# The first batch's keys and queries loaded as twelve rows a partition, in a block-sparse attention feeding a mixture of experts

## The chip, the cores and the metric

The kernel runs on one core of one Trainium2 chip. Its metric is the device time in microseconds of one execution, as the median of several runs. The core has five engines with a queue of instructions each: TensorE (PE in the profile, its weight loads PEld), VectorE (DVE), ScalarE (ACT), GpSimd (POOL), and SyncE (SP), which here issues most of the transfers. Transfers run on 16 DMA engines that all the queues share. A matmul writes to PSUM; ACT and DVE copy results from there to SBUF.

## What is computed

Attention over 4 batches of 8 heads, 768 positions of 64 elements, with a mask in blocks of 32 positions: a query block sees its neighbours, the first and last block, and three sampled blocks; the first and last query blocks see everything. The result, as 3,072 tokens of 512, goes to the best of 8 experts.

```python
scores = scale * np.matmul(q, k.transpose(0, 1, 3, 2))
mask = np.abs(blk_i - blk_j) <= window
mask = mask | (blk_i == 0) | (blk_j == 0) | (blk_i == n_blocks - 1) | (blk_j == n_blocks - 1)
for qb in range(n_blocks):
    for kb in sampled_blocks[qb]:
        mask[qb * block:(qb + 1) * block, kb * block:(kb + 1) * block] = True
attn = np.exp(np.where(mask, scores, -1e9) - max)   # and divided by its sum
x = np.matmul(attn, v)                              # to (tokens, 512)
expert = np.argmax(x @ w_gate, axis=1)
y = gate_weight * (np.maximum(x @ w1[expert], 0) @ w2[expert])
```

## The kernel before

The two halves follow one another: attention until about 280 us of the profiled execution, then the experts. In the attention each batch needs its keys and queries with the head's 64 elements on the partitions. They come from memory with positions on the partitions and are turned on TensorE. Two heads make a pair; a batch has four pairs (NPR), so 64 + 64 partitions hold the two heads of a pair.

`fill_stage` (L137) loads keys or queries of one pair into a staging buffer by two DMAs, one a head, each with position 128 c + p of chunk c on partition p; a partition gets six pieces of 64 fp32 elements (256 B each) a head. There are two staging slots for keys and two for queries, used by pairs in turn. `turn` (L150) makes twelve transposes of 64 positions by 128 columns (both heads at once) into a PSUM tile `tp` of two banks, and `turned` (L159, the copy at L161) copies 128x768 to the place where the pair's keys or queries lie, one instruction: on ACT for the first batch's keys, on DVE for its queries. The copy writes runs of 64 elements.

The first batch is brought in ahead of the regular steps. Its values come by `load_v` (L142, copies at L144): a DMA per head, also in pieces of 256 B. `keep_v` (L146, L148) writes them back to memory as whole rows of all heads (v_rows, 2,080 B a row), from which GpSimd gathers the sampled blocks' rows by indirect DMA (`fetch_values`, L488) and SP fetches the two end blocks (`fetch_ends`, L496). v_rows has to be complete before either reads it.

For the first and last query blocks, which see all keys, `scores(plan_all(0, pr))` multiplies (24 matmuls at L321), ACT takes the Exp (L331), and `attend_all` multiplies the result with the values (twelve second products a pair, L355) into an accumulator that the regular steps finish. `make_masks` (L243) makes the masks and the row numbers for the gathers (rows_of, L248; mask, L254) from four small matmuls. These PSUM tiles (tp, s, fl) share three buffers of two banks, in the order of allocation.

The order of all this is written out by hand: in this part of the program each engine executes in the order in which the code issues. Before, a loop over the pairs runs: turn keys, turn queries, load the pair two further on into the freed slot, (after the first pair) load the values' second half, (after the second pair) write v_rows and load the gate, scores and Exp of this pair, (after the second pair) masks, second products of the pair before. Twenty-two transposes of the identity (L240) at the very start keep TensorE busy until the first data are there.

The regular steps then take a query group and two pairs each; a step's scores need copies of the sampled keys (kr, L528) and end keys (xk, L512 and L513), and its second products need the gathered values (around). `not_before` (L500) paces the gathers.

Of the kernel before, what the change touches and what calls it, by code (L numbers as in the profile page):

```python
# [7 lines left out]
F32 = mybir.dt.float32  # L8
# [9 lines left out]
def kernel(  # L18
# [11 lines left out]
    nc = tc.nc  # L30
    P = 128
    B, H, S, D = q.shape
# [3 lines left out]
    NCH = S // P  # L36
    CW = NCH // 2 * P
    NPR = H // 2
# [32 lines left out]
    ident = const.tile([P, P], F32, name="ident")  # L71
# [14 lines left out]
    upper, lent = {}, ExitStack()  # L86
# [25 lines left out]
    def held(flat):  # L112
        a, c = NPR * S, 2 * NPR * S
        return (
            flat[:, :a].rearrange("p (r s) -> p r s", r=NPR), flat[:, a:c].rearrange("p (r s) -> p r s", r=NPR),
            flat[:, c : c + NCH * VR].rearrange("p (c w) -> p c w", c=NCH),
        )

    sets = [held(other[:]), held(room[:])]
    sets = [sets[(b + B - 1) % 2] for b in range(B)]  # L120
    at = 2 * NPR * S + NCH * VR
    stage = [[room[:, at + (2 * i + j) * S : at + (2 * i + j + 1) * S] for i in range(2)] for j in range(2)]
# [14 lines left out]
    def fill_stage(b, pr, which, slot=0):  # L137
        to = stage[which][slot].rearrange("p (c h d) -> p c h d", c=NCH, h=2)
        for hh in range(2):
            nc.sync.dma_start(to[:, :, hh, :], (k, q)[which][b, 2 * pr + hh].rearrange("(c p) d -> p c d", p=P))  # L140

    def load_v(b, hs=None):  # L142
        for h in range(H) if hs is None else hs:
            nc.sync.dma_start(sets[b][2][:, :, h * VW : h * VW + D], v[b, h].rearrange("(c p) d -> p c d", p=P))  # L144

    def keep_v(b, cs=None):  # L146
        for c in range(NCH) if cs is None else cs:
            nc.sync.dma_start(v_d[b][c * P : (c + 1) * P, :], sets[b][2][:, c, :])  # L148

    def turn(b, pr, which, on=None, slot=0):  # L150
        src = stage[which][slot].rearrange("p (c w) -> p c w", c=NCH)
        tp = upper["ps_s"].tile([P, 2, 512], F32, name="tp", tag="s")
        for c in range(NCH):
            for j in range(2):
                r = slice(j * D, (j + 1) * D)
                nc.tensor.transpose(tp[:, j, c * D : (c + 1) * D], src[r, c, :], ident[r, r])
        return lambda: turned(b, pr, which, on, tp)

    def turned(b, pr, which, on, tp):  # L159
        to = sets[b][which][:, pr, :].rearrange("p (c j t) -> p j c t", c=NCH, j=2)  # L160
        (on or nc.scalar.copy)(to, tp[:, :, : NCH * D].rearrange("p j (c t) -> p j c t", c=NCH))  # L161
# [81 lines left out]
    def make_masks(spread, whose, own, qb):  # L243
        fl = upper["ps_s"].tile([P, 2, 2, NTI], F32, name="fl", tag="s")
        for w in range(2):
            for ch in range(2):
                nc.tensor.matmul(fl[:, w, ch, :], lhsT=spread[:, w, ch, :], rhs=whose[:], start=True, stop=True)
        nc.vector.tensor_scalar(  # L248
            rows_of.rearrange("p (t c) -> p c t", c=2), fl[:, 0], scalar1=float(BLK), scalar2=qb[:, 2:3], op0=ALU.mult, op1=ALU.add,
        )  # L250
        for ch, p0 in ((0, D), (1, 0)):
            for ti in range(2):
                shape = [P - p0, NG - ti, 2, BLK]
                nc.vector.tensor_tensor(  # L254
                    mask[p0:, : NG - ti, 1 + ch, ti, :].rearrange("p t (a i) -> p t a i", a=2),
                    fl[p0:, 1, ch, ti::2].unsqueeze(2).unsqueeze(3).to_broadcast(shape),
                    own[p0:, ch, :].unsqueeze(1).unsqueeze(3).to_broadcast(shape), op=ALU.mult,
                )
# [6 lines left out]
        nc.gpsimd.memset(two.rearrange("p c (h w) -> p c h w", w=VW)[:, :, :, D], 1.0)  # L265
    for pr in range(2):
        for which in range(2):
            fill_stage(0, pr, which, pr)
    load_v(0, range(4))
    make_lists_pool = ExitStack()  # L270
    lists = make_lists(make_lists_pool.enter_context(tc.tile_pool(name="mk", bufs=1)))
    rt = {}
    xbs, xos, lgs, banks_of, es = {}, {}, {}, {}, {}
# [8 lines left out]
    def all_queries(b, pr):  # L282
        return lambda r: sets[b][1][:, pr, :].rearrange("p (n i) -> p n i", i=BLK)[r, :: NB - 1, :]

    def at_cols(tile_, a, n):
        return lambda r: tile_[r, a : a + n]
# [13 lines left out]
    def plan_all(b, pr):  # L300
        kT = sets[b][0][:, pr, :]
        return [(j, at_cols(kT, c * P + j * D, D), all_queries(b, pr), c * D, D) for c in range(NCH) for j in range(2)], []
# [11 lines left out]
    def scores(*plans):  # L314

        ss = [upper["ps_s"].tile([P, 2, 512], F32, name="s") for _ in plans]
        for s, (few, _) in zip(ss, plans):
            for j, keys, queries, a, n in few:
                for hh in range(2):
                    r = slice(hh * D, (hh + 1) * D)  # L320
                    nc.tensor.matmul(s[j * D : (j + 1) * D, hh, a : a + n], lhsT=keys(r), rhs=queries(r), start=True, stop=True)  # L321
        for s, (_, many) in zip(ss, plans):
            for keys, queries, a, n in many:
                for hh in range(2):
                    r = slice(hh * D, (hh + 1) * D)
                    nc.tensor.matmul(s[:, hh, a : a + n], lhsT=keys(r), rhs=queries(r), start=True, stop=True)  # L326
        found = []
        for s in ss:
            e = ea[:, units[0] % NE, :].rearrange("p (h w) -> p h w", h=2)
            units[0] += 1  # L330
            nc.scalar.activation(e, s[:, :, : 6 * D], AF.Exp, scale=scale)  # L331
            found.append(e)
        return found
# [18 lines left out]
    def product(b, g, pr, ti, hh, e, values, last):  # L352
        bank, begun = bank_of(b, g, pr)
        op = bank[:, : 4 * (D + 4)].rearrange("p (r h w) -> p r h w", r=2, h=2)
        nc.tensor.matmul(  # L355
            op[ti * D : (ti + 1) * D, pr % 2, hh, : D + 1], lhsT=e, rhs=values[:, (2 * pr + hh) * VW : (2 * pr + hh + 1) * VW],
            start=ti not in begun, stop=last, skip_group_check=True,
        )
        begun.add(ti)
# [12 lines left out]
    def attend_all(b, pr, e, chunks):  # L372
        for c in chunks:
            for hh in range(2):
                product(b, GL, pr, 1, hh, e[:, hh, c * D : (c + 1) * D], sets[b][2][:, c, :], c == NCH - 1)
# [9 lines left out]
            attend_all(b, pr, e_all, range(3, NCH))  # L385


    for pr in range(NPR):
        turn(0, pr, 0, None, pr % 2)()
        turn(0, pr, 1, nc.vector.tensor_copy, pr % 2)()  # L390
        if pr + 2 < NPR:
            fill_stage(0, pr + 2, 0, pr)
            fill_stage(0, pr + 2, 1, pr)
        if pr == 0:
            load_v(0, range(4, H))
        if pr == 1:
            keep_v(0)
            nc.sync.dma_start(wg[:], moe_w_gate.rearrange("(c p) e -> p c e", p=P))
        (es[("all", pr)],) = scores(plan_all(0, pr))
        if pr == 1:  # L400
            make_masks(*lists)
            make_lists_pool.close()
        if pr > 0:
            attend_all(0, pr - 1, es[("all", pr - 1)], range(NCH))
    attend_all(0, NPR - 1, es[("all", NPR - 1)], range(NCH))
    wp = ctx.enter_context(tc.tile_pool(name="wp", bufs=1))
    sm = ctx.enter_context(tc.tile_pool(name="sm", bufs=1))
    work = ctx.enter_context(tc.tile_pool(name="work", bufs=2))
# [194 lines left out]
    def attention_again():  # L603
        oh, pen = dense_tables(small)
        for b in range(B):
            for two in (sets[b][2],):
                nc.gpsimd.memset(two.rearrange("p c (h w) -> p c h w", w=VW)[:, :, :, D], 1.0)
            load_v(b)
            for pr in range(NPR):
                for which in range(2):  # L610
                    fill_stage(b, pr, which)
                    turn(b, pr, which)()
            for g in range(NG):
                for pr in range(NPR):
                    shifted(b, g, pr, oh, pen)
                    if pr % 2:
                        divide(b, g, pr // 2)
                turn_out(b, g)
                logits(b, g)
            gate(b)  # L620
            gate_weights()
# [913 lines left out]
```

## Time and profile before

| | us |
|---|---|
| median of three runs | 679.02 (676.74 to 680.68) |
| the profiled execution | 650.76 |
| its span, first to last instruction | 649.0 |
| TensorE busy, matmuls | 611.7 (94% of the span) |
| VectorE busy | 300.9 (46%) |
| ScalarE busy | 218.1 (34%) |
| TensorE busy in the first 35 us | 27.0 |
| DMA share and rate in the first 35 us | 0.94, 199 GB/s |

Durations below come from the profiled execution. A row of the timeline gives the start, the time that the merged instructions took, the engine and line, the tiles written and read, the count, and in brackets how long the engine had been idle and what ended it. Queues carry a q (SPq); a transfer's row there is its issue, not its data. A fp32 matmul shows as two instructions. The row of a stage gives its busy time per engine, the clock that TensorE was granted as a share of full speed, the mean busy share of the 16 DMA engines, and the rate.

### The profile page before, as it was taken

How to read it: one execution, taken by the hardware profiler on the slowest of the kernel's cores; microseconds unless marked ns; L12 is line 12 of the kernel's file. 1: busy time of each engine (PE TensorE's matmuls, PEld its weight loads, DVE VectorE, ACT ScalarE, POOL GpSimd, SP SyncE). 2: the span in 40 equal slices, each digit the busy share in tenths (PEclk: the TensorE clock that was granted, in tenths of full speed). 3: DMA queues.
4: the chain of work that ended last, by engine and by line, in shares of the span. 5: the costliest groups of instructions: out<-in, count | busy, mean ns of one | idle time of the engine just before them, and what ended most of it. 6: DMA issues, size and time to landing. Idle time of an engine off the chain costs nothing. (4 is left out here: it accounts for less than half of the span.)

```text
span 649.0 us, 21354 instructions
## 1 busy us (share of the span) xinstructions
PE 611.7 (94%) x8952; PEld 512.0 (79%) x8952; DVE 300.9 (46%) x966; ACT 218.1 (34%) x418; POOL 184.1 (28%) x289
## 2 busy tenths in 40 slices
PE   7789999998999997999999999999989999999994
PEld 6778888997999886987777777877869678867862
DVE  4247765765577488734920495202091024602200
ACT  2347755775677655431111011111111211111110
POOL 2047753552455344620111221011400212020210
PEclk9689999999999999699999999999999999999998
DMA  9889886987797338876888999869995799989950
GB/s 184 210 195 245 243 218 158 221 231 198 158 232 235 95 90 290 283 260 231 315 299 299 335 383 348 293 239 382 396 397 192 256 405 397 339 278 402 396 189 20
DMA packets 136249, 170.93 MB, mean 263 GB/s; under 512 B 83444, under 2 KB 83445, under 8 KB 136118
## 3 DMA queue, kind: packets, MB, share of 16 engines
q1 hardware_dynamic: 126080, 137.61, 65.4%
q0 software_dynamic: 10000, 31.59, 15.2%
q8 instruction: 80, 1.31, 0.9%
q14 instruction: 51, 0.42, 0.2%
q10 hardware_dynamic: 38, 0.00, 0.0%
HBM read 150.11 MB, written 19.33 MB: 261 GB/s over the span
## 5 line engine op out<-in xcount | busy, mean ns | idle before, releaser
L1094 PEld LDWEIGHTS hp<-around,room 128*128 128x128 f32 x1216 | 138.3, 192 | 7.3 <-issue 5.1
L1094 PE MATMUL hp<-around,room 128*128 128x128 f32 x1216 | 140.8, 276 | 1.4 <-ACT kr L1101 1.4
L1075 DVE STREAM_TRANSPOSE around<-xg 32x128 f32<-32x128 f32 x208 | 63.0, 303 | 125.9 <-PE hp L1094 95.9
L1108 PE MATMUL zp<-room,kr 128*128 128x512 f32 x256 | 112.7, 594 | 0.0
L488 POOL DMA_INDIRECT around<-v_rows,rows_of x88 | 92.6, 1052 | 63.5 <-DVE xk L513 25.3
L331 ACT ACTIVATE ea<-s 128x768 f32<-128x768 f32 x104 | 79.7, 809 | 91.1 <-PE s L326 70.7
L355 PE MATMUL op<-around,ea 128*64 128x65 f32 x2112 | 87.6, 228 | 5.2 <-DMA around<-v_rows,rows_of 3.9
L1108 PEld LDWEIGHTS zp<-room,kr 128*128 128x128 f32 x256 | 47.6, 191 | 54.6 <-issue 54.6
L355 PEld LDWEIGHTS op<-around,ea 128*64 128x64 f32 x2112 | 76.3, 140 | 13.3 <-DMA around<-v_rows,rows_of 4.5
L337 DVE TENSOR_TENSOR ea<-ea,mask 128x768 f32<-128x768 f32 x80 | 73.2, 954 | 14.8 <-ACT ea L331 14.8
L1101 ACT ACTIVATE kr<-hp 128x512 f32<-128x512 f32 x36 | 21.5, 597 | 117.4 <-PE hp L1094 109.9
L1123 POOL DMA_INDIRECT out_dram<-kr,sB x14 | 14.1, 1005 | 164.7 <-ACT kr L1113 106.1
L1113 ACT ACTIVATE kr<-zp,xg 128x512 f32<-128x512 f32 x16 | 11.0, 687 | 101.2 <-PE zp L1108 101.2
L1201 DVE STREAM_TRANSPOSE ea<-ea 32x128 f32<-32x128 f32 x84 | 21.7, 285 | 32.7 <-DMA ea<-x_rows,gB 32.0
L321 PE MATMUL s<-room 64*64 64x64 f32 x736 | 24.4, 237 | 5.3 <-DVE room L161 4.6
L1123 POOL DMA_INDIRECT out_dram<-kr,sA x5 | 5.1, 1020 | 79.6 <-ACT kr L1113 79.6
L326 PE MATMUL s<-other,kr 64*128 64x64 f32 x352 | 26.9, 266 | 0.7 <-issue 0.7
L321 PEld LDWEIGHTS s<-room 64*64 64x64 f32 x736 | 20.2, 147 | 7.3 <-issue 4.5
L326 PE MATMUL s<-room,kr 64*128 64x64 f32 x352 | 25.8, 261 | 0.0
L326 PEld LDWEIGHTS s<-other,kr 64*128 64x128 f32 x352 | 25.0, 195 | 0.8 <-issue 0.8
L326 PEld LDWEIGHTS s<-room,kr 64*128 64x128 f32 x352 | 23.9, 190 | 1.0 <-issue 1.0
L500 POOL COPY paced<-sums 1x1 f32<-1x1 f32 x42 | 7.5, 179 | 60.1 <-DVE sums L415 55.6
(338 smaller groups left out, 870.2 us busy)
## 6 DMA issues: line engine op xcount, KB each, us to landing
room<-in_moe_w_dram SPq DMA_DIRECT2D x46, 2048.0 KB
room<-in_moe_w_dram SPq DMA_DIRECT2D x16, 512.0 KB
room<-in_k_dram SPq DMA_DIRECT2D x32, 192.0 KB
room<-in_q_dram SPq DMA_DIRECT2D x32, 192.0 KB
x_rows<-xb SPq DMA_DIRECT2D x20, 256.0 KB
v_rows<-room SPq DMA_DIRECT2D x12, 260.0 KB
v_rows<-other SPq DMA_DIRECT2D x12, 260.0 KB
room<-in_v_dram SPq DMA_DIRECT2D x16, 192.0 KB
```

The costliest lines, as they stand in the source:

```text
L321: nc.tensor.matmul(s[j * D : (j + 1) * D, hh, a : a + n], lhsT=keys(r), rhs=queries(r), start=True, stop=True)
L326: nc.tensor.matmul(s[:, hh, a : a + n], lhsT=keys(r), rhs=queries(r), start=True, stop=True)
L331: nc.scalar.activation(e, s[:, :, : 6 * D], AF.Exp, scale=scale)
L337: nc.vector.tensor_tensor(e, e, m[:, None, :].to_broadcast([P, 2, 6 * D]), op=ALU.mult)
L355: nc.tensor.matmul(op[ti * D : (ti + 1) * D, pr % 2, hh, : D + 1], lhsT=e, rhs=values[:, (2 * pr + hh) * VW : (2 * pr + hh + 1) * VW], sta ...
L488: nc.gpsimd.indirect_dma_start(out=around[p0:, par, 1 + ti + 2 * ch, :], out_offset=None, in_=v_d[b][:, :], in_offset=bass.IndirectOffsetO ...
L1075: nc.vector.transpose(xT[d, :, t], xg[t, :DM].rearrange("p (c q) -> p c q", c=DB)[:, :, d])
L1094: nc.tensor.matmul(hp[:, m, :], lhsT=st[i]["w1"][:, c, fb * P : (fb + 1) * P], rhs=st[i]["xT"][:, c, :], start=(c == 0), stop=(c == DB - 1),)
L1101: nc.scalar.activation(hT[:, g * (FB // 2) : (g + 1) * (FB // 2), :], hp[:], AF.Relu)
L1108: nc.tensor.matmul(zp[:], lhsT=st[i]["hT"][:, fb, :], rhs=st[i]["w2"][:, fb, :], start=(fb == 0), stop=(fb == FB - 1),)
L1123: ins = nc.gpsimd.indirect_dma_start(out=to[:, :], out_offset=bass.IndirectOffsetOnAxis(ap=at, axis=0), in_=rows, in_offset=None, bounds_c ...
L1201: nc.vector.transpose(xT_u[d, :, j * P + tq * 32 : j * P + (tq + 1) * 32], xg_u[t, j, :DM].rearrange("p (c q) -> p c q", c=DB)[:, :, d],)
```

## The change

The first batch's keys and queries are loaded otherwise, turned otherwise, and the order of the opening is another. Later batches keep `fill_stage` and `turn`.

A pair's two heads lie in memory one after the other, so the whole pair is one contiguous block. `fill_rows` loads it by one DMA: partition h * 64 + i takes positions 12 i to 12 i + 11 of head h, 768 elements or 3,072 B in one piece. `turn_rows` again makes twelve transposes of 64 by 128, now one for each head and each two neighbouring positions, so that a PSUM bank holds one head: the even position's elements on partitions 0 to 63, the odd one's on 64 to 127. Four copies of 64x384 put them in the order of positions: bank 0 (the first head) by ACT, bank 1 by DVE, even and odd each. A copy reads PSUM with a step of 64 elements (six of them, then the next) and writes to SBUF with a step of two elements.

```diff
+    KG = S // D
+
+    def fill_rows(b, pr, which, slot):
+
+        nc.sync.dma_start(stage[which][slot], (k, q)[which][b, 2 * pr : 2 * pr + 2].rearrange("h (i j) d -> (h i) (j d)", j=KG))
+
+    def turn_rows(b, pr, which, slot):
+        src = stage[which][slot]
+        tp = upper["ps_s"].tile([P, 2, 512], F32, name="tp", tag="s")
+        for hh in range(2):
+            r = slice(hh * D, (hh + 1) * D)
+            for j in range(KG // 2):
+                nc.tensor.transpose(tp[:, hh, j * D : (j + 1) * D], src[r, j * P : (j + 1) * P], ident[r, r])
+        for hh, copy in enumerate((nc.scalar.copy, nc.vector.tensor_copy)):
+            to = sets[b][which][hh * D : (hh + 1) * D, pr, :].rearrange("p (i j a) -> p a i j", j=KG // 2, a=2)
+            for a in range(2):
+                copy(to[:, a], tp[a * D : (a + 1) * D, hh, : KG // 2 * D].rearrange("p (j i) -> p i j", i=D))
...
-            fill_stage(0, pr, which, pr)
+            fill_rows(0, pr, which, pr)
...
-    for pr in range(NPR):
-        turn(0, pr, 0, None, pr % 2)()
-        turn(0, pr, 1, nc.vector.tensor_copy, pr % 2)()
+    def turn_first(pr):
+
+        for which in range(2):
+            turn_rows(0, pr, which, pr % 2)
         if pr + 2 < NPR:
-            fill_stage(0, pr + 2, 0, pr)
-            fill_stage(0, pr + 2, 1, pr)
-        if pr == 0:
+            for which in range(2):
+                fill_rows(0, pr + 2, which, pr)
+        if pr == 1:
             load_v(0, range(4, H))
-        if pr == 1:
             keep_v(0)
             nc.sync.dma_start(wg[:], moe_w_gate.rearrange("(c p) e -> p c e", p=P))
+
+    def scores_first(pr):
         (es[("all", pr)],) = scores(plan_all(0, pr))
-        if pr == 1:
-            make_masks(*lists)
-            make_lists_pool.close()
-        if pr > 0:
-            attend_all(0, pr - 1, es[("all", pr - 1)], range(NCH))
-    attend_all(0, NPR - 1, es[("all", NPR - 1)], range(NCH))
+
+    turn_first(0)
+    turn_first(1)
+    scores_first(0)
+    turn_first(2)
+    scores_first(1)
+    turn_first(3)
+    make_masks(*lists)
+    make_lists_pool.close()
+    scores_first(2)
+    scores_first(3)
+    for pr in range(NPR):
+        attend_all(0, pr, es[("all", pr)], range(NCH))
```

On TensorE the opening becomes: turns of pairs one and two, scores of one, turns of three, scores of two, turns of four, the masks' matmuls, scores of three and four, then the second products of all four pairs. On SP it becomes: keys and queries of pairs one and two, the first half of the values, keys and queries of pairs three and four, the second half of the values, v_rows, the gate, the end blocks; before, the second half of the values stood ahead of pair four's keys and queries. In the program as built, DVE's first copy of a turn carries a wait for ACT's two copies of that turn, and every SP transfer carries a wait for the completion of the transfer eight before it, as it did before.

## The prediction

> **What bounds the kernel now.** I read the page's slices first, then stages in the windows view, then the opening in the timeline, the sync engine's own timeline, and the vector engine's groups kept apart by shape.
>
> The slices (40 of 16.2 us) say where a saving would count:
>
> ```profile
> PE   7789999998999997999999999999989999999994
> PEclk9689999999999999699999999999999999999998
> DMA  9889886987797338876888999869995799989950
> ```
>
> TensorE is the bound nearly everywhere, so whatever makes its dense stretch begin earlier moves everything behind it. The exception is the opening: slices one to three at 7, 7, 8. The change touches only that. Stages of it (columns: stretch, length, busy us and count of PE, PE loads, DVE, ACT, POOL, then granted clock, DMA share, GB/s):
>
> ```profile
> 5.00:9.00 4.00, 2.85 (x57) 2.41 (x59) 2.86 (x13) 0.80 (x1) 0.68 (x4) 1.00 1.37 220
> 13.50:14.50 1.00, 1.00 (x6) 1.00 (x5) 0.00 (x0) 0.48 (x1) 0.00 (x0) 0.50 0.29 63
> 14.50:22.50 8.00, 6.50 (x100) 5.91 (x101) 3.12 (x6) 1.03 (x2) 0.00 (x0) 0.50 1.16 225
> 24.50:27.50 3.00, 1.17 (x24) 0.96 (x24) 0.79 (x1) 0.80 (x1) 0.00 (x0) 0.93 1.05 385
> 30.00:31.50 1.50, 1.50 (x16) 1.50 (x16) 0.93 (x6) 1.25 (x5) 0.38 (x1) 0.50 0.00 0
> ```
>
> Until 23 us the DMA engines are full but move only 220 to 225 GB/s: these are the loads of q, k and v in pieces of 256 B. The writes of v_rows (2,080 B a row) move 385. Then DMA is empty while a completion is awaited. The timeline names the chain:
>
> ```profile
> 20.36 2.33 SPq L140 DMA_DIRECT2D room<-in_q_dram  x2
> 22.97 3.56 SPq L148 DMA_DIRECT2D v_rows<-room  x6
> 29.30 5.12 PE L355 MATMUL op<-room,ea 128*64 128x65 f32 x48
> 30.29 1.20 SPq L496 DMA_DIRECT2D around<-v_rows  x2
> 31.12 1.17 POOL L488 DMA_INDIRECT around<-v_rows,rows_of  x1 [25.31 <-DVE xk L513]
> 32.60 0.92 POOL L488 DMA_INDIRECT around<-v_rows,rows_of  x1 [0.30 <-issue]
> 37.82 0.45 PE L355 MATMUL op<-around,ea 128*64 128x65 f32 x4 [0.54 <-DVE ea L341]
> 40.20 2.01 PE L355 MATMUL op<-around,ea 128*64 128x65 f32 x20 [1.94 <-DMA around<-v_rows,rows_of]
> ```
>
> Two chains meet at 40.20. The value chain: loads, then v_rows written from about 23.4, complete at 30.29, gathers on POOL from 31.12, the second of them landing 6.7 us after its issue ends (33.5 to 40.2). The TensorE chain: last second products until 34.42, scores of the first two steps, Exp, mask, ready at 37.82. TensorE then waits 1.94 us for the gather. So the value chain binds, with about 2 us of slack in the other.
>
> [...] here data of v_rows thins out at 28.8 us and its waiter goes at 30.29, 1.5 us. [...] (columns: busy us, mean ns):
>
> ```profile
> L716 DVE TENSOR_TENSOR selA<-sc,best 128x144 f32<-128x144 f32 x1 | 0.4, 403 | 0.0
> L784 DVE TENSOR_REDUCE slA<-slot 128x18 f32<-128x144 f32 x1 | 0.4, 401 | 0.0
> L712 DVE TENSOR_TENSOR sc<-sc,first_w 128x144 f32<-128x144 f32 x1 | 0.3, 308 | 0.0
> L714 DVE TENSOR_REDUCE best<-sc 128x18 f32<-128x144 f32 x1 | 0.3, 303 | 0.0
> ```
>
> L716 writes and L784 reads at a step of 72 bytes; L712 and L714 are the same sizes without a step: 95 and 98 ns more over 144 elements, 0.66 to 0.68 ns an element. [...]
>
> **The change, part by part.**
>
> *Loads.* Sixteen loads of 192 KB in 256 B pieces become eight of 384 KB in pieces of 3,072 B. No trace row has this load; the nearest is the 2,080 B write, 385 GB/s. Bounds: 300 (slices of the weight phase on the page fall that low) to 397 (its best). Taken: 385. The old loads: 16 + 8 (v) x 196.6 KB = 4.72 MB between 2.0 and 23.2 us, 223 GB/s with gaps. New: q and k 3.15 MB / 385 = 8.2 us, v 1.57 MB / 225 = 7.0 us; from 2.0 they end at 17.2, if no gap opens. As built, a load waits for the completion of the one eight before it; [...]. Eight in flight now carry more bytes, and the waits of the third and fourth pairs on the turns (turn done 7.0 to 10.5 by the sum below) come before their data's turn on the queue (9 to 13), so I expect no gap.
>
> *v_rows.* Moved on SP from behind the last q load to directly behind the last v loads. It now has to see these complete: 1.5 us plus some 0.6 us to first data: writes start at 17.2 + 2.1 = 19.3, not 23.4. That is 4.1 us earlier; the drained queue is the price, already in it. The gate load, the two end fetches, batch two's loads on SP and POOL's gathers follow it in the same order as before, 4.1 us earlier: first gathered product at 40.2 - 4.1 = 36.1.
>
> *Copies.* Per pair: one ACT copy of 128x768 (805 ns) and one DVE copy (957 ns) become four of 64x384 on each. ACT: from 587 ns at 512 and 805 at 768, 0.85 ns an element, so 0.48 us unstepped. DVE: 166 ns at 8 (L459) and 957 at 768, so 0.56 us. [...] the PSUM read at a step of 256 bytes is in no row. Low end: no penalty, 0.56 and 0.48. High end: the SBUF penalty twice, DVE 0.56 + 2 x 384 x 0.68 ns = 1.1, ACT 0.9. Taken: once on DVE, 0.8; ACT 0.55. As built, DVE's two copies of a turn also wait for ACT's two, and all three PSUM tiles wait for both, so a turn is 1.1 then 1.6 us, pipelined at DVE's pace.
>
> *TensorE's chain.* The same 96 transposes, 96 score matmuls and 48 second products (each matmul two instructions in the trace). Running it forward from 6.47 us (unchanged: the 22 warm-up transposes end there): DVE's copies of pair one end at 11.4, pair two 14.6, pair three 18.2, pair four 22.0; scores of the fourth to 23.3; then all second products in one piece, 96 instructions at 107 ns (5.12 us / 48, at a clock mostly of 0.50) or half of that at full clock; with the clock rising on the way I take 80: 7.7 us, to 31.0. Before: 34.42. Plus the same 3.4 us to ready: 34.4, ahead of the gather at 36.1. So the copies' extra 16 x 0.8 - 4 x 0.96 = 9 us of DVE and 16 x 0.55 - 4 x 0.8 = 5.6 us of ACT are hidden by the value chain, and TensorE's products lying idle until the end cost nothing as long as TensorE is ready by 36.1.
>
> *Masks.* Their four matmuls and 2.2 us on DVE move behind the last copy, 22.0 to 24.4; the gathers need rows_of at 26, hidden.
>
> Sum: -4.1 us. Span 649.0 to 644.9, this execution's own 650.76 to 646.7. The median of the runs, 679.02, lies 28.3 us above the profiled execution; the profile doesn't show where, and I carry the saving over in microseconds: 674.9.
>
> **Rivals.** *TensorE's chain takes over, or the loads run at 300 GB/s.* At 300 q and k take 10.5 us, the gain shrinks to 1.8; at 1.0 us a DVE copy TensorE is ready near 37, gain 3. [...] Result: 676 to 678.5.
>
> *Stepped copies are dear (slower).* One mechanism: DVE's read of PSUM at 256 bytes a step. Everything before the second products then runs at DVE's pace, sixteen copies in line. From 1.15 us a copy (3 ns an element) the value chain's gain is gone; at 1.6 us the sixteen need 26 us, last scores near 36, second products to 43, ready at 46.5 against 40.2: 685. For: no such read in the trace [...]. Against: the SBUF penalty is only 0.68 ns an element; that would have to be threefold.
>
> *More than the value chain.* If the loads reach 397 [...]: gain 6 to 8, 672.
>
> **How the numbers follow.** Half a per cent, 3.4 us, is about what can be told from no change. Main case, chance 0.50, its own range 673 to 677: 0.42 of it beyond 3.4 us, 0.08 within. Takeover or slow loads 0.22, within. Dear copies 0.20, slower. More 0.08. So faster 0.50, same 0.30, slower 0.20; the range 669 to 683 leaves out the worst of the dear copies and the run scatter at the low end.
>
> **What would show it.** Right: loads in the first 6 us near 385 GB/s; v_rows issued near 19, the end fetches near 26.2, first gathered product near 36; DVE copies under 1 us. Wrong: copies above 1.15 us; second products ending after 34.4; a gap in DMA before 17 us; or the 4 us lost again before 100 us.

## The result, and the profile after

The changed kernel takes 675.62 us (median of 20 runs), the kernel before 679.06 us (20 runs beside them): ratio 0.9947, 95% interval 0.9925 to 0.997. It was run again twice, each time beside the kernel before on one chip: 651.00 against 652.09 us, ratio 0.9983 (0.9956 to 1.001), and 675.39 against 677.57 us, ratio 0.9964 (0.9937 to 0.9991). So it is faster by 1.1 to 3.4 us, on average about 2.2, where 4.1 were forecast; taken alone, the second of the three comparisons can't be told from no change. The medians given are of all runs, while the ratios and their intervals use only the faster of two states into which the executions fall, so a ratio can differ from the quotient of the two medians beside it.

One caution before any lines are compared. The profiled execution of the changed kernel took 676.08 us, that of the kernel before 650.76. The chips differ by that much with one and the same kernel (652, 678 and 681 us for the kernel before on the three chips below). So I read the opening from the changed kernel's second profile, which I call the repeat (655.09 us, span 653.4, on the chip where the kernel before has 652.09), against the lines of before that the prediction shows. These are single profiles; where others of the same two kernels differ, it is said.

The slices of the changed kernel's first profile (40 of 16.9 us), TensorE, its clock, DMA:

```profile
PE   7979999999999998889999999999999999999995
PEclk8779899999988999968999999999999999999998
DMA  9579776877685425882788999878996699979960
```

Slice two is dense now, but slice three is still at 7, and the clock of slices two and three is below full (7 tenths). The DMA share of the second slice has fallen from 8 to 5, because more of the loading falls into the first one (267 GB/s, 184 before).

The sync engine, POOL and TensorE in the repeat's timeline (columns: start us, length us, engine, line, operation, and in brackets the idle time before it with what ended it):

```profile
13.17 3.87 SPq L162 DMA_DIRECT2D room<-in_v_dram  x1
20.06 4.43 SPq L166 DMA_DIRECT2D v_rows<-room  x6
23.16 6.96 PE L373 MATMUL op<-room,ea 128*64 128x65 f32 x96
28.67 1.21 SPq L523 DMA_DIRECT2D around<-v_rows  x2
29.51 1.17 POOL L515 DMA_INDIRECT around<-v_rows,rows_of  x1 [23.71 <-DMA v_rows<-room]
30.99 0.93 POOL L515 DMA_INDIRECT around<-v_rows,rows_of  x1 [0.30 <-issue]
34.86 0.42 PE L373 MATMUL op<-around,ea 128*64 128x65 f32 x4 [1.87 <-DVE ea L359]
37.51 2.43 PE L373 MATMUL op<-around,ea 128*64 128x65 f32 x20 [2.24 <-DMA around<-v_rows,rows_of]
40.17 0.18 DVE L444 RECIPROCAL r<-sums 128x4 f32<-128x4 f32 x1
```

The same chain binds as before. The second products end at 30.1 (before 34.42), TensorE is ready for the first gathered products at 34.86 (before 37.82), and it waits 2.24 us for the gather, 37.51 in place of 40.20. The gain at that point is 2.7 us in this pair of profiles. The changed kernel's two other profiles have 39.34 and 36.94 there and the kernel before's second 39.81, so the lead is anything from 0.5 to 3.3 us. Most of that spread is the gather's own: from the end of its issue to the product it took 5.6 us in the repeat, 7.9 and 6.1 in the two others, 6.7 and 6.0 in the kernel before.

The repeat in stretches (columns: stretch, length, busy us and count of PE, PE loads, DVE, ACT, POOL, then granted clock, DMA share, GB/s):

```profile
2.00:6.00 4.00, 4.00 (x24) 3.83 (x22) 2.85 (x12) 1.25 (x2) 3.32 (x15) 1.00 0.92 308
17.00:17.50 0.50, 0.50 (x8) 0.33 (x5) 0.26 (x1) 0.23 (x1) 0.00 (x0) 0.50 0.83 145
17.50:19.00 1.50, 1.49 (x15) 1.38 (x15) 0.42 (x1) 1.30 (x3) 0.00 (x0) 0.50 0.78 167
19.50:20.50 1.00, 1.00 (x9) 0.97 (x13) 0.95 (x3) 0.19 (x1) 0.00 (x0) 0.50 0.00 0
22.50:23.00 0.50, 0.50 (x28) 0.50 (x22) 0.50 (x2) 0.33 (x1) 0.00 (x0) 0.50 0.06 8
23.50:24.00 0.50, 0.50 (x8) 0.50 (x7) 0.47 (x4) 0.50 (x1) 0.00 (x0) 0.50 0.95 354
```

Data of the loads thin out at 17 and, but for a small rest, end at 19. Nothing moves while the completion is awaited (0 GB/s from 19.5 to 20.5). Then, in the middle of the writes of v_rows, a hole of about a microsecond opens (8 GB/s at 22.5). The copies are cheap (from the first profile; the repeat agrees to 1 ns; columns: busy us, mean ns, then the idle time before them):

```profile
L158 ACT COPY room<-tp 64x384 f32<-64x384 f32 x16 | 8.0, 498 | 5.8 <-PE tp L154 5.7
L158 DVE COPY room<-tp 64x384 f32<-64x384 f32 x16 | 8.9, 556 | 4.0 <-ACT room L158 3.6
```

### The profile page after: what moved, and what is told of

It reads as the page before. It is cut to its first block, busy times and chain, and to the rows that moved or that the text cites. A ratio compares the mean times of both kernels' runs of the same rounds, so it can differ in the third digit from the quotient of the medians.

```text
span 674.3 us, 21380 instructions
## 1 busy us (share of the span) xinstructions
PE 631.2 (94%) x8952; PEld 525.4 (78%) x8952; DVE 306.4 (45%) x978; ACT 223.2 (33%) x430; POOL 184.0 (27%) x289
## 5 line engine op out<-in xcount | busy, mean ns | idle before, releaser
L515 POOL DMA_INDIRECT around<-v_rows,rows_of x88 | 91.5, 1040 | 59.1 <-DMA v_rows<-room 23.3
L373 PE MATMUL op<-around,ea 128*64 128x65 f32 x2112 | 94.0, 236 | 7.8 <-DMA around<-v_rows,rows_of 3.2
L373 PEld LDWEIGHTS op<-around,ea 128*64 128x64 f32 x2112 | 81.9, 148 | 16.8 <-issue 7.6
L344 PE MATMUL s<-room,kr 64*128 64x64 f32 x352 | 29.9, 261 | 3.5 <-issue 3.1
L344 PEld LDWEIGHTS s<-room,kr 64*128 64x128 f32 x352 | 26.3, 188 | 5.5 <-issue 5.5
L344 PE MATMUL s<-other,kr 64*128 64x64 f32 x352 | 29.3, 273 | 0.8 <-issue 0.6
L344 PEld LDWEIGHTS s<-other,kr 64*128 64x128 f32 x352 | 27.0, 201 | 1.3 <-issue 1.2
L339 PE MATMUL s<-room 64*64 64x64 f32 x736 | 25.8, 245 | 1.3 <-issue 0.9
L344 PE MATMUL s<-room,xk 64*128 64x128 f32 (+1 forms) x192 | 24.4, 307 | 2.3 <-issue 2.1
```

The source lines that it names most:

```text
L373: nc.tensor.matmul(op[ti * D : (ti + 1) * D, pr % 2, hh, : D + 1], lhsT=e, rhs=values[:, (2 * pr + hh) * VW : (2 * pr + hh + 1) * VW], sta ...
L515: nc.gpsimd.indirect_dma_start(out=around[p0:, par, 1 + ti + 2 * ch, :], out_offset=None, in_=v_d[b][:, :], in_offset=bass.IndirectOffsetO ...
```

## The experiments

Twelve runs on three chips; the ratio is always to the kernel before on the same chip. Edits are shown against the kernel named.

**Which half of the change brings the gain?** First the kernel before itself, as the null; then each half of the change alone; then the whole.

*The kernel before, again* (no edit).

> The kernel before, unchanged, to have its trace from the same chip as the runs beside it. Every theory: ratio 1.000 within 0.003. The two profiles at hand differ by 25 us between 60 and 290 us of the span, where the change touches nothing; if that is the chip and not the change, this profile's execution lies near 679 us and reaches 60 us and 290 us as late as the changed kernel's did (within some 3 us), and no longer 25 us earlier.

Measured 653.01 us, ratio 1.0015 (0.999 to 1.0041). That is what no change looks like here. The 679 us that I expected of its profile could not come: this chip is a faster one. That the 25 us lie with the chip is shown the other way round, by the changed kernel at 651.00 us on this chip and at 675 on two others.

*Long rows, old order*: the new loads, turns and stepped copies, in the order of the kernel before on every engine and queue.

```diff
-    turn_first(0)
-    turn_first(1)
-    scores_first(0)
...
+        (es[("all", pr)],) = scores(plan_all(0, pr))
+        if pr == 1:
+            make_masks(*lists)
+            make_lists_pool.close()
+        if pr > 0:
+            attend_all(0, pr - 1, es[("all", pr - 1)], range(NCH))
```

> Long rows and stepped copies, but the order of the opening as before: the second half of the values ahead of pair four's keys and queries, second products between the scores. Value-chain theory: v_rows no longer waits for a drained queue, so it is complete near 24 us against 30.3 before and 28.2 in the changed kernel; TensorE's last second products end near 29; the first gathered product comes 4 to 6 us earlier than before; ratio 0.992 to 0.994, at least as fast as the whole change. Rival, that the order of TensorE's work is what gains: ratio 0.998 to 1.000.

Measured 656.74 us, ratio 1.0069 (1.0042 to 1.0095): slower, and my expectation fell. The value chain did what it should: v_rows issued at 17.87, end fetches at 24.12, six microseconds ahead of before. But it no longer decides. Pair four on TensorE's timeline:

```profile
29.28 1.14 PE L154 MATMUL tp<-ident,room 64*128 64x64 f32 x24
32.14 0.47 PE L339 MATMUL s<-room 64*64 64x64 f32 x2 [1.72 <-ACT room L158]
33.45 1.55 PE L339 MATMUL s<-room 64*64 64x64 f32 x46 [0.84 <-DVE room L158]
34.93 4.88 PE L373 MATMUL op<-room,ea 128*64 128x65 f32 x48
```

From turn to scores stand ACT's four copies and behind them DVE's four, and TensorE has nothing to do meanwhile. The waits view sums this up for TensorE from 5 to 36 us, the run with long rows and then the kernel before on the same chip (columns: what waited, for what, total us, times, longest):

```profile
PE s L339 <- ACT room L158: 6.9, 4, 1.7
PE s L339 <- DVE room L158: 3.7, 4, 1.0
```

```profile
PE s L321 <- DVE room L161: 4.6, 4, 1.1
PE tp L156 <- DMA room<-in_q_dram: 3.2, 4, 1.2
PE tp L156 <- DMA room<-in_k_dram: 1.1, 1, 1.1
```

10.6 us of waiting for copies against 4.6 us. The waits for data, 4.3 us in that profile of before, are gone. The second products end at 39.8 instead of 34.4, and the gather has landed long before.

*Old loads, new order*: the old loads, turns and single copies, in the new order.

```diff
-            fill_rows(0, pr, which, pr)
+            fill_stage(0, pr, which, pr)
...
-        for which in range(2):
-            turn_rows(0, pr, which, pr % 2)
+        turn(0, pr, 0, None, pr % 2)()
+        turn(0, pr, 1, nc.vector.tensor_copy, pr % 2)()
```

> Short pieces and the single copies as before, but the new order. Value-chain theory: loads end at 23 as before, the values' second half is now last, so v_rows waits for its completion and is written 2 us later than before; all second products come after the last scores; first gathered product 2 to 4 us later than before; ratio 1.003 to 1.006. Rival, that the order gains: ratio 0.995 to 0.997.

Measured 654.61 us, ratio 1.0038 (1.0011 to 1.0064): slower, as the value chain says, though by little: the interval of no change above reaches 1.0041. Second products end at 30.7, as early as in the changed kernel, and TensorE stands idle for it:

```profile
25.76 3.93 SPq L166 DMA_DIRECT2D v_rows<-room  x6
33.18 1.20 SPq L523 DMA_DIRECT2D around<-v_rows  x2
39.49 0.67 PE L373 MATMUL op<-around,ea 128*64 128x65 f32 x4 [5.93 <-DMA around<-v_rows]
42.02 2.43 PE L373 MATMUL op<-around,ea 128*64 128x65 f32 x20 [1.86 <-DMA around<-v_rows,rows_of]
```

The new order puts the values last on SP, so v_rows waits for the end of all loads: 2.8 us later than before.

*The changed kernel, again* (no edit).

> The changed kernel, unchanged, beside the others on their chip. Ratio 0.995 (0.992 to 0.997), as measured. Value-chain theory: first gathered product 1 to 4 us earlier than in the kernel before on this chip, and the same lead still there at 100, 200 and 290 us. Rival, that the gain arises later in the attention: no lead at 60 us and a lead that grows.

Measured 651.00 us, ratio 0.9983 (0.9956 to 1.001); its profile is the repeat shown above. What became of the lead that I expected to last is told with the table of the divides below. Each half alone makes the kernel slower; together they make it a little faster (on this chip by no more than the interval). The order covers the copies, and the long rows make up for the order's late values.

**Is the gather still what binds, and can its wait be removed?**

*All values first*: the second half of the value loads joins the first, ahead of the last two pairs.

```diff
-    load_v(0, range(4))
+    load_v(0)
...
-            load_v(0, range(4, H))
```

> The changed kernel with one edit: all eight value loads are issued ahead of the keys and queries of the last two pairs, so the copies to v_rows no longer have to wait for the last loads of the queue; TensorE's order is that of the changed kernel. Theory 'the value chain still binds, because v_rows waits for the last load': v_rows is issued near 17.5 us, the end fetches go near 25, the gather is no longer waited for, and the first gathered products start when TensorE's own chain is ready, 2 us earlier than in the changed kernel; ratio to before about 0.993, 0.003 below the changed kernel's on the same chip. Rival 'TensorE's chain is as late as the gather': ratio within 0.001 of the changed kernel's, first gathered products at the same time. Rival 'the last pairs, now loaded later, hold TensorE': second products end after 31 us, ratio 1.00 or above.

Measured 686.01 us, the kernel before 680.82, ratio 1.0023 (0.9989 to 1.0057). The gather wait is gone, and the last of the rivals decided instead:

```profile
16.33 1.15 PE L154 MATMUL tp<-ident,room 64*128 64x64 f32 x12 [5.24 <-DMA room<-in_k_dram]
31.03 8.07 PE L373 MATMUL op<-room,ea 128*64 128x65 f32 x96
42.49 2.64 PE L373 MATMUL op<-around,ea 128*64 128x65 f32 x24 [0.53 <-DVE ea L359]
```

TensorE waits 5.24 us for pair three's keys (1.66 in the repeat), and everything behind is late; the second products take 8.07 us (6.96 in the repeat).

*The values in the middle*: the second half behind pair three, ahead of pair four only. That is where SP had it before the change.

```diff
-        if pr == 1:
+        if pr == 0:
             load_v(0, range(4, H))
+        if pr == 1:
             keep_v(0)
```

> The changed kernel with one edit: the second half of the value loads is issued ahead of the last pair's keys and queries only (behind the third pair's), so that the copies to v_rows need not wait for the last loads; TensorE's order is unchanged. Theory 'the gather wait in the changed kernel comes from the drained queue': v_rows issued near 18 us, end fetches near 24.5, gathers land near 33, ahead of TensorE's own chain (35 to 36 us), so the first divide comes 1.5 to 2 us before the changed kernel's and the ratio is 0.002 to 0.003 below it. Rival 'batch two's loads and the gathers, now earlier, [...]': second products take 8 us or more instead of 7, first divide no earlier, ratio 0.000 to 0.008 above the changed kernel's.

Measured 678.00 us, the kernel before 677.57, ratio 0.9993 (0.9963 to 1.0024): no gain is left that can be seen, though the interval overlaps that of the changed kernel on this chip (0.9937 to 0.9991). The value side came as expected (v_rows issued 18.43, end fetches 24.68, no wait for the gather). TensorE's side gave it back:

```profile
19.49 2.11 PE L154 MATMUL tp<-ident,room 64*128 64x64 f32 x24 [2.37 <-DMA room<-in_k_dram]
28.63 0.35 PE L373 MATMUL op<-room,ea 128*64 128x65 f32 x3 [0.35 <-issue]
30.09 6.15 PE L373 MATMUL op<-room,ea 128*64 128x65 f32 x75 [1.11 <-issue]
39.63 1.61 PE L373 MATMUL op<-around,ea 128*64 128x65 f32 x24 [0.53 <-DVE ea L359]
```

Pair four's turn waits 2.37 us for its data, and the second products take 10.1 us (26.1 to 36.2) in place of 7, with pauses that end on nothing the profile shows ("issue"). They fall together with the loads of batch two, which SP starts at 25.99 here and at 29.98 in the repeat; that those loads cause the pauses is not shown. Long rows in the old order start them at 25.42, on the fastest of the three chips, and the second products beside them have no such pause.

*All values first, and second products between the turns*: the loads as above, and on TensorE two pairs' products in the holes.

```diff
+    scores_first(1)
+    attend_first(0)
     turn_first(2)
-    scores_first(1)
+    attend_first(1)
     turn_first(3)
...
+    attend_first(2)
+    attend_first(3)
```

> The loads of the last experiment, and TensorE's order changed as well: turns 1 and 2, scores 1 and 2, second products of pair 1, turn 3, second products of pair 2, turn 4, masks, scores 3 and 4, second products of pairs 3 and 4. Theory: half of the second products now fill TensorE's idle time between the second and the fourth turn, so they end near 27 us instead of 30; then the gather (landing near 34) is late again by 1 to 2 us and binds; first gathered products near 34; ratio to before 0.988 to 0.992. Rival 'products in between delay the turns and their serial copies, as in the old order': second products end after 30 us, ratio no better than that of the changed kernel (0.997 to 1.000).

Measured 683.02 us against 680.82, ratio 1.0034 (1.0008 to 1.006). The same program once more:

> The version with all values first and second products between the turns, once more. In its first run the first divide came 2 us before the changed kernel's, but the median was 5.7 us above it on the same chip. Theory 'the loss is real, from later in the attention stage': ratio again 0.006 to 0.010 above the changed kernel's, with the first divide early. Rival 'one chip's scatter': ratio 0.002 to 0.004 below the changed kernel's.

Measured 679.92 us against 677.57, ratio 1.0001 (0.9974 to 1.0029). In both profiles the first divide (of the first finished accumulator, just behind the gathered products) comes at 38.4 to 38.5, the earliest of all, and yet the medians are not better than before. On the second chip the ratio lies 0.0037 above the changed kernel's own, 0.9964; the theory had expected 0.006 to 0.010, its rival a ratio below, and neither came. The changed kernel itself was not run on the first of the two chips; its version with filled idle time (below) had 0.9947 there. That the early divide brings no gain was seen twice, but its cause I could not settle; what the traces say of it follows below.

**How much slack does TensorE have in the changed kernel?**

*Idle time filled*: 14 transposes of the identity ahead of the third turn.

```diff
+            if pr == 2:
+                idle = ps_o.tile([P, 512], F32, name="lay", tag="op")
+                for c in range((6, 8)[which]):
+                    nc.tensor.transpose(idle[:, :P], ident[:], ident[:])
             turn_rows(0, pr, which, pr % 2)
```

> The changed kernel with 14 transposes of the identity added ahead of the third turn, where TensorE stands idle for data. They compute nothing that is used. They test whether TensorE's clock or pace in the opening matters: theory 'the gather binds': second products end at most 1 us earlier or later, the first gathered products stay within 0.5 us of the changed kernel's, ratio to the changed kernel within 0.002. Rival 'TensorE's clock binds': the gathered products start 1 us or more earlier, or run faster, ratio 0.003 lower.

Measured 677.37 us against 680.82, ratio 0.9947 (0.9921 to 0.9973). The added work delayed the last turns, second products ended at 30.8, and TensorE still waited 1.45 us for the gather. The gain is that of the changed kernel elsewhere; the changed kernel itself was not run on that chip.

*Work added at the end of the opening*: 32 transposes behind the last second products.

```diff
+    late = upper["ps_s"].tile([P, 2, 512], F32, name="idle", tag="s")
+    for c in range(32):
+        nc.tensor.transpose(late[:, 0, :P], ident[:], ident[:])
```

> The changed kernel with 32 transposes of the identity added between the last second products of the opening and the scores that follow. They compute nothing that is used; 22 such transposes took 4.4 to 4.7 us in the opening, [...]. This measures what a microsecond in the opening is worth. Theory 'value chain binds with 2 us of slack in TensorE's, and what is left over is carried to the end in full': added 3.4 to 6.8 us, first divide later by that less 2 us (1.4 to 4.8 us), and the median later by the same, ratio 0.002 to 0.007 above the changed kernel's. Rival 'the opening is absorbed later': ratio within 0.001 of the changed kernel's.

The yardstick on the same chip was the changed kernel once more:

> The changed kernel itself once more, as the yardstick for the three others on the same chip. So far its ratio to before was 0.9947 and 0.9983. Theory 'gain of 2 to 3 us at the first divide, carried to the end': 0.9945 to 0.9985. Rival 'no gain, chip or placement': 1.000 or above.

Measured 675.39 us for the yardstick, ratio 0.9964, and 677.13 us with the added work, ratio 0.9959 (0.9935 to 0.9983). The 32 transposes took 3.71 us, more than the 2 us of slack that I had counted. By the ratios they cost nothing; the plain medians differ by 1.7 us, and the intervals are about that wide to either side, so a cost of that size could hide there:

```profile
29.99 3.71 PE L435 MATMUL idle<-ident 128*128 128x128 f32 x32
37.09 1.80 PE L373 MATMUL op<-around,ea 128*64 128x65 f32 x24 [0.53 <-DVE ea L359]
39.12 0.18 DVE L447 RECIPROCAL r<-sums 128x4 f32<-128x4 f32 x1
```

The first gathered products no longer wait for the gather, and 24 of them take 1.80 us, where the repeat needs 2.43 us for 20. So the first divide is not later at all (39.12; 39.60 in the yardstick, 40.17 in the repeat). The clock goes with it. The stretches 33 to 37 and 37 to 46 us in the kernel before, the repeat, and this run, in that order:

```profile
33.00:37.00 4.00, 4.00 (x79) 3.73 (x79) 0.20 (x1) 1.06 (x3) 1.43 (x2) 0.89 0.93 227
37.00:46.00 9.00, 6.52 (x106) 5.94 (x105) 4.87 (x14) 4.13 (x11) 4.28 (x6) 0.81 0.69 163
```

```profile
33.00:37.00 4.00, 0.42 (x4) 0.31 (x4) 1.85 (x5) 2.40 (x6) 2.78 (x5) 0.87 0.72 159
37.00:46.00 9.00, 8.49 (x103) 8.14 (x104) 3.99 (x10) 2.99 (x6) 1.66 (x3) 0.50 0.80 197
```

```profile
33.00:37.00 4.00, 3.56 (x71) 3.05 (x69) 0.92 (x1) 1.80 (x5) 0.16 (x1) 1.00 0.56 148
37.00:46.00 9.00, 8.39 (x180) 7.73 (x182) 6.06 (x19) 5.52 (x12) 4.86 (x8) 1.00 0.83 197
```

In the repeat TensorE is early, and so idle just ahead of the gather: 0.42 us busy out of 4. The clock then stands at 0.50 for the nine microseconds that follow, and 103 instructions run in them; with the idle stretch filled it stays at 1.00, and 180 run. The repeat's stretch is not idle throughout (its pauses are 1.87 and 2.24 us), and what brings the clock down is not shown.

Two things limit this. With the work added the half clock comes later instead, and by the fourth divide the lead over the yardstick is down from 2.6 us to 0.5:

```profile
52.50:56.00 3.50, 3.50 (x57) 3.38 (x56) 1.92 (x2) 2.88 (x6) 0.09 (x1) 0.54 1.14 277
```

And the kernel before can lose its clock in the same place. Its second profile, from the repeat's chip (execution 659.25 us), waits 2.45 us for the gather; 37 to 46 us:

```profile
37.00:46.00 9.00, 6.55 (x84) 6.17 (x86) 3.72 (x13) 2.60 (x6) 4.27 (x6) 0.58 0.80 178
```

So where the clock falls varies from one execution to the next, and that the change is what cost it in the repeat is not shown.

**Was it the wait between the two copying engines?**

*Long rows, old order, copies split by tensor*: ACT copies all of a pair's keys, DVE all of its queries, so that neither waits for the other within a turn.

```diff
-        for hh, copy in enumerate((nc.scalar.copy, nc.vector.tensor_copy)):
+        copy = (nc.scalar.copy, nc.vector.tensor_copy)[which]
+        for hh in range(2):
```

> Long rows in the old order once more, but ScalarE copies all of a pair's keys and VectorE all of its queries, so that no copy of one engine waits for one of the other within a turn. Theory 'in the old order the serial copies are the price': ScalarE's 2 us and VectorE's 2.2 us a pair run beside each other, the second products end 2 to 4 us earlier than the 39.8 us of the run without the split, the first divide 2 to 3 us earlier than 45.06; ratio to before 0.999 to 1.004 instead of 1.007. Rival 'the pauses come from loads or PSUM tiles': no change, ratio 1.006 or above.

Measured 685.79 us against 680.82, ratio 1.0065 (1.004 to 1.009): no better than 1.0069. TensorE's waits for copies fell from 10.6 to 8.4 us, but the second products ended at 40.6 and the first divide came at 45.88. So the crossing wait is at most a small part:

```profile
PE s L340 <- DVE room L159: 8.4, 8, 1.3
```

All of it is now waiting for DVE. What is left in the old order is that four small copies in line (2.2 us on DVE) stand between a turn and its scores with no other work there. Why the 2.2 us fewer of waiting brought no earlier end is not shown; this chip is one of the slower ones.

## Why the prediction was right, and where its sum was off

*The binding chain: right.* The gather bound before (a wait of 1.94 us) and binds after (2.24 us). Removing its wait in two ways moved the limit to TensorE's loads and products; adding 3.71 us to TensorE's side did not delay the first divide. That the gather takes as long from issue to product as before was taken, and is not true of single profiles (5.6 us in the repeat, 6.7 before). By this luck the first waited product came at 37.51, 1.4 us behind the forecast's 36.1, though the end fetches came 2.5 us behind.

*Loads: partly wrong.* The first pieces came at 308 GB/s (repeat, 2 to 6 us) and 331 (first profile), against 385 taken and 231 before in the same stretch. (The upper bound was misread: the page's best slice has 405 GB/s, not 397. On 3.15 MB either saves 0.2 to 0.4 us against 385, so the last rival's gain of 6 to 8 us doesn't follow from the loads; it was my estimate.) The term that failed is "loads end 17.2, no gap": they end at 19, 1.8 us later. The last value load of the second half took 3.87 us to issue on SP (13.17 to 17.04), and the last 250 KB move only after 17.5. The last one of the first half took 4.07 us, so pair three's keys were issued at 8.73 and TensorE waited 1.66 us for them, a wait that the sum had at nothing. In the kernel before no value load took over 1.02 us, but a key load of pair three took 2.38 (from 11.21), and behind it comes the gap of 13.5 to 14.5 (63 GB/s). What held these issues, no view shows; for the last value load of the first half it can't be the wait for the transfer eight before, since that load is SP's eighth.

*v_rows: mis-sized.* The step said: writes from 19.3, end fetches 26.2, so 4.1 us earlier at the end. Measured in the repeat: issued at 20.06 where "near 19" was forecast, and then 8.6 us to the end fetches at 28.67, where the sum has some 7.2 and the kernel before 7.3 (22.97 to 30.29). So the end fetches come 1.6 us earlier, not 4.1. About 1.1 us of the difference is the late loads, 1.4 us the six writes themselves. One of these was 2.10 us in issue, and this is the hole at 22.5:

```profile
20.93 2.10 SPq L166 DMA_DIRECT2D v_rows<-room  x1
```

In all five profiles of the changed kernel and of its two versions with work added, one of these writes takes 1.4 to 2.1 us to issue; with the old loads in the new order, where v_rows also stands right behind the values, one takes 1.61. In long rows with the old order and in the values in the middle, where pair four's loads stand between the values and v_rows, none takes over 0.7 us, and the six are complete 6.3 us after the first issue. The price of the drained queue was in the sum; this price of issuing right behind the value loads was not.

*Copies: cheaper than taken.* DVE 556 ns (taken 800), ACT 498 (taken 550): the unstepped rates of the sum. The rival of dear copies is out. The unstepped rates are estimates from the copies of before, as the prediction has them. The PSUM read at 256 bytes with the write at 8 bytes came within 18 ns of them (556 against 560 on DVE, 498 against 480 on ACT).

*TensorE's chain: right.* Forecast: second products end 31.0, ready 34.4. Measured 30.1 and 34.9 in the repeat. Its 96 instructions of second products took 72 ns each (6.96 us), where 80 were taken; in the kernel before they took 107 at a mean clock of 0.55 (29.3 to 34.4 us), and those of 100 to 110 us took 42 at 1.00. In part two misses cancel here: the cheaper copies of pair four ended at 20.9, 1.1 us before the sum's 22.0, and the scores behind them took that back (end 23.2, sum 23.3). The copies are hidden in this order; in the old one they are not, and TensorE's chain takes over, as the first rival describes it.

*What came back later: the clock.* TensorE's mean clock over the first 60 us is 0.83 in both profiles of the kernel before, and 0.83, 0.80 and 0.80 in the three of the changed kernel. An estimate from these means, with the clock taken as either 1.00 or 0.50: half clock for about 20 us before and about 24 us in two of the three profiles after; 4 us more at half clock are 2 us of work. The clock is at 0.50 also where TensorE is busy all the time: in two of the prediction's stages of before (1.00 us of 1.00 at 13.5, 1.50 of 1.50 at 30).

Starts of the divides in us, worked out from the timelines (first profile and repeat are the changed kernel's, the yardstick its third; the kernel before's second profile is from the repeat's chip):

```
divide  before  before,2nd  repeat | first prof.  yardstick  values_middle  work added  mixed, again
1        42.45       42.46   40.17 |       42.01      39.60          41.48       39.12         38.39
2        47.34       49.42   47.01 |       46.92      46.82          48.03       44.78         43.47
3        52.69       54.76   52.35 |       53.13      52.17          52.24       49.53         50.03
4        56.60       58.69   56.27 |       57.11      57.62          59.76       57.15         54.06
12       96.73       99.16   96.19 |      101.19     103.94         106.89      103.56         99.36
25      168.41      173.43  167.46 |      175.80     182.46         183.88      178.87        177.02
32      201.35      206.93  201.27 |      215.80     221.33         222.93      217.23        216.91
45      274.32      279.58  274.12 |      293.60     301.21         300.20      294.32        297.32
48      286.29      294.66  288.57 |      311.33     315.92         314.43      306.69        316.58
```

The columns left of the bar are of faster executions, those right of it of the slower chips, and single profiles scatter by microseconds towards the end. Against the first profile of before, the repeat's lead of 2.3 us at the first divide is 0.3 at the third, 0.5 at the twelfth and a lag of 2.3 at the last, which would be the prediction's own "4 us lost again before 100 us" in small. Against the second it is 2.4 at the third, 3.0 at the twelfth and 6.1 at the last. Neither is the steady lead that I expected. The two profiles of before part between divides one and two, where the second one's mean clock is 0.58 (37 to 46 us; the first one's 0.81). So the traces show a gain of 0.4 to 2.9 us at the first divide, over all pairs of profiles, and not how much of it reaches the end; that the medians gain 1.1 to 3.4 us is known from the runs alone.

So direction, binding chain and TensorE's side held; the single term of 4.1 us came out as 1.6 us at the end fetches and 2.7 at the first waited product of the repeat, and how much of it is carried is not shown. That the forecast of 674.9 lies so near the first measured 675.6 is partly luck: the two other comparisons give 1.1 and 2.2 us.

*Left open.* Whether a lead in the opening is carried to the end. Work added behind the second products brought divides two and three 2.0 and 2.6 us ahead of the yardstick's on the same chip, but at the fourth 2.2 of that was lost again, and its median is no better. The mixed version still leads on its chip at the 25th and 32nd divide and then needs 19.3 us for the last three, where the others on its chip need 12.4 to 14.7. Its first run (19.4) and all values first (19.5) show the same; but so, almost, does the changed kernel's first profile (17.7). In that stretch of the mixed version's second run, ACT's Exp waits long for something that the trace doesn't name:

```profile
303.07 0.81 ACT L349 ACTIVATE ea<-s 128x768 f32<-128x768 f32 x1 [6.16 <-remote]
```

What that is, no run here tells. No version tried that alters the order of its work beats the changed kernel.

## What to carry to other kernels

Price a move in a queue by what it makes the next item wait for: putting the values last drained the queue, and v_rows then paid for the wait until they were complete (their data end at 19, the first write was issued at 20.06) and for a slow issue besides (2.10 us for one write). A cheaper load and a new order can each be slower alone and faster together, when one opens the waits that the other fills; test both halves before believing in either. When a chain gets ahead, look at what TensorE does in the time won: in one profile a stretch of four microseconds with 0.42 us of work was followed by nine at a clock of 0.50. Filling such a stretch moved the low clock to a later place (0.54 from 52.5 to 56 us) and gained nothing in the median. And take a second profile of the kernel before on the same chip before a lead, or its loss, is explained: here the two disagree by 2 us at the second divide.

## What the runs showed of the hardware

A PSUM read at a step of 256 bytes with an SBUF write at a step of 8 bytes runs at about the unstepped rate: 556 ns on VectorE and 498 on ScalarE for 64x384, where the rates of the copies of before give an estimate of 560 and 480.

An SP issue that mostly takes 0.35 to 0.65 us can take far longer with no wait shown beside it: the last of four value loads in 256-byte pieces 3.2 to 4.7 us in the changed kernel's three profiles, and one write of v_rows shortly behind such loads 1.4 to 2.1 us.

TensorE can pause with no wait that the profile shows. From 60 to 280 us such pauses before L344 add up to 1.6 us in the repeat, and to 7.5 us in the run with idle time filled, on a chip where the kernel before is 29 us slower (before all lines 7.1 and 13.1 us, so they are not most of the 29). Line one is of the repeat, line two of the other:

```profile
PE s L344 <- issue: 1.6, 3, 0.6
```

```profile
PE s L344 <- issue: 7.5, 21, 0.5
```

The granted clock fell to half in the repeat behind a stretch that was not idle throughout: 37 to 46 us at 0.50, behind 33 to 37 us at 0.87 with pauses of 1.87 and 2.24 us and 0.42 us of work. In two profiles of one and the same kernel (before) the stretch from 37 to 46 us had a mean clock of 0.81 and 0.58.
